# Second MoE block: six float32 weight pieces parked in DRAM, more of the small tensor work on VectorE, a new listed order

## The chip, the cores and the metric

The kernel runs on one core of a Trainium2 chip. TensorE (PE) multiplies, ScalarE (ACT), VectorE (DVE) and GpSimd (POOL) do the element-wise work, and SyncE (SP) issues every DMA in one queue. The metric is the device time of one execution in microseconds, the median over runs. For the kernel before it is 686.53 us (three runs, 686.2 to 686.76).

## The reference

Three blocks follow each other: a windowed attention over 2304 tokens (four sequences of 512 local and 32 global tokens, 8 heads of 64), a first MoE block (512 to 1024 to 512, softmax gate and layer norm), and the second block, which the change touches:

```python
def _moe2_ref(x, w_in, w_out):          # x (2304, 512), w_in (512, 2048), w_out (2048, 512)
    h = x @ w_in
    neg, pos = h <= -1.0, h >= 1.0
    g = np.where(pos, h, np.where(neg, 0.0, (h + 1.0) ** 2 / 4.0))
    return (g @ w_out).astype(np.float32)
```

## The kernel before

**Precision.** A float32 matrix is held as two parts: a high part, which ScalarE copies out in the matmul's own rounding, and a low part, the difference, which VectorE or GpSimd subtracts (`sub`, L835). A product is then three matmuls (`mm3`, L319): high by high, high by low, low by high. So each operand of TensorE needs one ScalarE copy and one or two subtractions first.

**Tiling of the second block.** The tokens form three blocks of 768, 768 and 640 (`BLOCKS`). The 2048 inner columns are 16 pieces `f` of 128 columns; each has an input weight `w2["i", f]` and an output weight `w2["o", f]`. For block 0 the pieces 0 to 7 are multiplied directly, each in two halves (`hprod`, L765; the loop over `k` at L1258). From piece 8 on, and for all of blocks 1 and 2, two pieces are taken together as a *pair* (`pair`, L902): a Strassen-Winograd scheme with seven products instead of eight. I write pair (b, p) for block b and pieces 2p and 2p+1. So there are four pairs in block 0, (0, 4) to (0, 7), and eight in each of the blocks 1 and 2. A pair needs

- four sums of token quarters, once per block (`ysum`, L840), with high and low parts (`yhigh`, `ylow`);
- four sums of weight quarters: `wfull` (L857) rebuilds the two float32 pieces into the tile `wt` by adding their high and low parts, `wsum` (L863) forms the sums in place, `whigh` and `wlow` split them into the tiles `S`. These sums are made once for each p, while the pair ahead of its first use runs, stored in DRAM (`wstore`) and loaded again for later blocks;
- seven products on two PSUM banks in turn, after which VectorE merges a product with earlier ones (`merge`, L929). The bank is free for the next product but one when its merge has read it. The activation is two ScalarE instructions and one on VectorE (`bend`, `least`), then the copy and the subtraction for `g`.

Between the seven products TensorE does the twelve accumulations `acc<-wo,g` of the pair before. The weights arrive as float64 words: each piece is fetched to `wraw` and converted by the steps A (ScalarE), B, D, F (VectorE) into the float32 tile `w32` (three buffers), then H (ScalarE) and L (VectorE or GpSimd) give its two parts (`conv`, L222).

**What sets the order.** The second block first lists its ScalarE, VectorE, GpSimd, DMA and matmul steps in `plan` (`later` appends). `ORDER`, a table of numbers at the head of the file, then calls them in a chosen order, so each engine's queue is in that order and each engine works in order. Which engine does a subtraction is fixed in the code before: GpSimd for `wfull`, `wlow`, nearly every low part of `g`, and the first four `ysum` (L1187), which are issued ahead of the plan.

Of the kernel before, what the change touches and what calls it, by code (L numbers as in the profile page):

```python
# [1439 lines left out]
```

## Time and profile before

| | us |
|---|---|
| median of three runs | 686.53 |
| the profiled execution | 686.77 |
| its span, first to last instruction | 684.6 |
| PE busy in the span | 655.7 (96%) |
| DVE, ACT, POOL busy | 446.7, 382.4, 277.1 |
| second block's direct stage, 301.89 to 363.29 | 61.40 |
| five pairs (0, 4) to (1, 0), 363.29 to 456.99 | 93.70 |

The profile is one execution. Times in it are counted from the span's start, and about 2.2 us of the execution lie outside the span. "Idle before <-" after an instruction is the time its engine stood still ahead of it and the engine that ended the wait. Neighbouring instructions of one engine overlap by some 0.07 us in the records, so from one start to the next is the better measure of what an instruction costs its queue. A pair is bounded here by the starts of its first product.

### The profile page before, as it was taken

The page shows a single profiled execution, that of the slowest core. Times are in us where ns is not written, and L with a number is a line of the kernel's source. Part 1 is how long each engine was busy: PE and PEld are TensorE (multiplying, and loading weights), DVE is VectorE, ACT ScalarE, POOL GpSimd, SP SyncE. Part 2 cuts the span into 40 slices and gives each one's busy share as a digit, 9 for nine tenths or more (in the row PEclk, how much of TensorE's full clock was granted, in tenths as well). Part 3 has the DMA queues.
Part 4 walks back from the last instruction along what each step waited for, and adds up shares of the span by engine and source line. Part 5 has one row for each costly group of instructions (what it writes and reads, how often), then busy time and mean ns, then how long its engine had stood idle before and what let it go on. Part 6 is the DMA issues. An engine that isn't in the chain of part 4 may idle for free.

```text
span 684.6 us, 15083 instructions
## 1 busy us (share of the span) xinstructions
PE 655.7 (96%) x6068; PEld 574.7 (84%) x6068; DVE 446.7 (65%) x746; ACT 382.4 (56%) x925; POOL 277.1 (40%) x286
## 2 busy tenths in 40 slices
PE   7699999999999999999999899799999999999997
PEld 4477889889898898989997788699998998988986
DVE  6998988785777499546999779955323353333332
ACT  5888886674564163428665556455434466444443
POOL 2243432141112143246677768866422254222321
PEclk9999999999999999999999999899999999999999
DMA  8999644336365335002574364244533335734512
GB/s 342 411 360 363 231 156 172 108 107 269 126 220 183 126 109 199 1 1 91 190 269 168 93 237 165 96 163 160 185 123 123 123 125 203 247 135 154 179 67 78
DMA packets 30837, 117.38 MB, mean 171 GB/s; under 512 B 3504, under 2 KB 4016, under 8 KB 28208
## 3 DMA queue, kind: packets, MB, share of 16 engines
q1 hardware_dynamic: 30768, 116.42, 47.6%
q8 instruction: 48, 0.79, 0.5%
q14 instruction: 21, 0.17, 0.1%
HBM read 92.03 MB, written 24.38 MB: 170 GB/s over the span
## 4 chain that ended last, share of the span: by engine, by line
PE 72%; DVE 12%; POOL 6%; issue 4%; DMA 3%; ACT 2%; SPq 0%; POOLq 0%; ACTq 0%; DVEq 0%
PE acc L324 19%; PE h L324 18%; PE h L583 12%; PE yT L324 10%; PE o L486 3%; PE S L405 2%; DVE xy L196 2%; DVE w L234 2%; PE pPT L471 2%; PE plnT L648 2%; POOL g L836 2%; DMA qkT<-in_qk_dram 2%; POOL S L836 1%; DVE w L236 1%; DVE w L232 1%
## 5 line engine op out<-in xcount | busy, mean ns | idle before, releaser
L324 PE MATMUL acc<-wo,g 128*128 128x512 f32 x816 | 214.6, 395 | 3.1 <-ACT o L205 3.1
L324 PEld LDWEIGHTS acc<-wo,g 128*128 128x128 f32 x816 | 150.3, 189 | 25.7 <-ACT o L205 3.4
L836 POOL TENSOR_TENSOR g<-xy,g 128x384 fp32r<-128x384 f32 (+2 forms) x95 | 92.4, 977 | 161.0 <-ACT g L205 135.5
L583 PE MATMUL h<-win,x 128*128 128x512 f32 x408 | 101.4, 400 | 1.1 <-issue 1.1
L205 ACT ACTIVATE xy<-xy 128x384 f32<-128x384 f32 (+1 forms) x148 | 74.7, 505 | 48.1 <-DVE xy L196 43.3
L324 PE MATMUL yT<-lnT,wout 128*128 128x256 f32 x768 | 95.7, 284 | 1.1 <-DVE lnT L196 1.0
L324 PEld LDWEIGHTS yT<-lnT,wout 128*128 128x128 f32 x768 | 92.9, 188 | 2.3 <-DVE lnT L196 1.5
L583 PEld LDWEIGHTS h<-win,x 128*128 128x128 f32 x408 | 74.8, 188 | 18.3 <-issue 1.9
L196 DVE SCALAR_TENSOR_TENSOR xy<-xy 128x384 f32<-128x384 f32 (+1 forms) x60 | 37.4, 623 | 51.3 <-ACT xy L205 51.3
L205 ACT ACTIVATE g<-xy 128x384 fp32r<-128x384 f32 (+1 forms) x88 | 44.3, 503 | 39.7 <-DVE xy L196 38.6
L196 DVE TENSOR_TENSOR xy<-h,xy 128x384 f32<-128x384 f32 (+1 forms) x80 | 42.2, 528 | 35.7 <-PE h L324 34.2
L324 PE MATMUL h<-yT,w2i 128*128 128x384 f32 (+1 forms) x324 | 61.9, 335 | 0.0
L324 PEld LDWEIGHTS h<-yT,w2i 128*128 128x128 f32 x324 | 57.2, 190 | 3.1
L324 PE MATMUL h<-yT,S 128*128 128x384 f32 (+1 forms) x240 | 46.5, 328 | 3.7 <-DVE xy L196 3.7
L205 ACT ACTIVATE xy<-h 128x384 f32<-128x384 f32 (+1 forms) x48 | 22.6, 470 | 48.9 <-PE h L324 48.8
L205 ACT ACTIVATE e<-S,nm 128x128 f32<-128x128 f32 x128 | 45.1, 380 | 7.6 <-DVE nm L196 5.7
L324 PE MATMUL h<-yc,S 128*128 128x384 f32 (+1 forms) x240 | 46.7, 330 | 1.7 <-DVE xy L196 1.4
L324 PEld LDWEIGHTS h<-yT,S 128*128 128x128 f32 x240 | 41.3, 188 | 8.1 <-DVE xy L196 4.8
L324 PEld LDWEIGHTS h<-yc,S 128*128 128x128 f32 x240 | 41.7, 191 | 6.3 <-DVE xy L196 3.0
L571 POOL TENSOR_TENSOR x<-xy,x 128x512 fp32r<-128x512 f32 x17 | 22.3, 1317 | 36.0 <-ACT x L205 29.9
L196 DVE SCALAR_TENSOR_TENSOR xy<-h,xy 128x384 f32<-128x384 f32 (+1 forms) x28 | 14.9, 534 | 30.9 <-ACT xy L205 30.9
L234 DVE SCALAR_TENSOR_TENSOR w<-wraw,w 128x512 int32<-128x512 int32 x38 | 33.5, 883 | 0.8
(153 smaller groups left out, 1042.4 us busy)
## 6 DMA issues: line engine op xcount, KB each, us to landing
vw<-in_vwin_dram SPq DMA_DIRECT2D x16, 1024.0 KB, 6.2
wo<-w2d_o SPq DMA_DIRECT2D x32, 512.0 KB, 4.1
S<-w2d_s SPq DMA_DIRECT2D x24, 512.0 KB, 5.1
qkT<-in_qk_dram SPq DMA_DIRECT2D x15, 768.0 KB, 7.0
wraw<-in_w2i_dram SPq DMA_DIRECT2D x16, 512.0 KB, 5.8
wraw<-in_w2o_dram SPq DMA_DIRECT2D x16, 512.0 KB, 4.1
w2d_o<-wo SPq DMA_DIRECT2D x16, 512.0 KB, 2.9
w2d_s<-S SPq DMA_DIRECT2D x16, 512.0 KB, 4.8
```

Of the source, the lines that this page charges most:

```text
L196: self.last = getattr(nc.vector, name)(*args, **kw)
L205: vec.act = nc.scalar.activation(**kw)
L232: return nc.vector.tensor_scalar(w.t, w.t, 3, None, ALU.logical_shift_left)
L234: return nc.vector.scalar_tensor_tensor(out=w.t, in0=w.high, scalar=SIGN, in1=w.t, op0=ALU.bitwise_and, op1=ALU.bitwise_or)
L324: mm(out=dst, lhsT=pairs[i][0][x], rhs=pairs[i][1][y], start=start and j == 0, stop=stop and j == 3 * n - 1, **kw)
L405: mm(out=S[32 * hp:32 * hp + 32, par, ci], lhsT=qT[r, hp, ci], rhs=kT[r, hp, w:w + 4].rearrange("p c d -> p (c d)"), start=True, stop=True)
L471: nc.tensor.transpose(ps[:, hp], eT[t][:, HP * par + hp], ident)
L486: mm(out=o[rows, ci, par], lhsT=PT[t][:, par, ci, rows], rhs=w[:, ci, D * h:D * h + D], start=True, stop=True)
L571: eng.tensor_tensor(out=xT[t][1], in0=x[:, :, n:n + P], in1=xT[t][0].bitcast(F32), op=ALU.subtract)
L583: mm(out=hps[t][:, half], lhsT=x[i][:, k], rhs=win[j][:, k, sl], start=not lo and j == 0 and k == 0, stop=lo and k == KD - 1)
L648: nc.tensor.transpose(ps[:, k], ln[t][:, P * c:P * c + P], ident)
L836: eng.tensor_tensor(out=out, in0=x, in1=y, op=ALU.subtract)
```

## The change

Four things change, all in the second block.

1. **Kept weights.** Input pieces of the sums that are converted inside the plan (10 to 15) have their float32 tile `w32` stored to DRAM after step F (`wkeep`). Where the sums of the pairs (0, 5), (0, 6) and (0, 7) are made, `wfetch` loads each piece into `wt` by one DMA of 256 KB instead of two GpSimd additions.
2. **A free choice of engine.** `ylow`, `wfull`, `wsum`, `wlow`, the low parts of `g` and of the weights are listed one instruction at a time, and an entry of `ORDER` may end in `v` (VectorE) or `p` (GpSimd).
3. **Whole halves.** In the direct stage the low part of `g` is one instruction of 128x384 instead of two of 128x192.
4. **The order.** A new table, and the four `ysum` of block 0 are entries of it.

On VectorE this gives 823 instructions instead of 740, on GpSimd 182 instead of 291, on SyncE 233 instead of 221. TensorE's order is the same row for row, and ScalarE has the same 767 instructions in another order.

```diff
 ORDER = """
-22 57 0 92 1 2 10 3 36 123 4 24 11 6 13 53 5 142 37 25 12 38 15 17 39 28 14 7 41 16 32 8 27 20 23 18 30 29 19
+25 60 4 95 5 6 0v 13 7 1v 9 109p 8 39 27 15 110p 14 18 10 17 16 40 11v 28 41 19 20 31 42 22 26 21v 44 36 30 32
...
-    def wfull(p, i):
+    def wfull(p, i, j, eng=nc.gpsimd):
         wt[p] = wts[0]
         a, b = w2["i", 2 * p + i]
-        for j in range(2):
-            nc.gpsimd.tensor_tensor(out=wt[p][:, 2 * i + j], in0=a[:, 2 * j:2 * j + 2].bitcast(F32), in1=b[:, 2 * j:2 * j + 2].bitcast(F32), op=ALU.add)
+        eng.tensor_tensor(out=wt[p][:, 2 * i + j], in0=a[:, 2 * j:2 * j + 2].bitcast(F32), in1=b[:, 2 * j:2 * j + 2].bitcast(F32), op=ALU.add)
+
+    def wfetch(p, i):
+        wt[p] = wts[0]
+        dma(out=wt[p][:, 2 * i:2 * i + 2].rearrange("p a k n -> p (a k n)"), in_=w2d["f", 2 * p + i])
+
+    def wkeep(f, w):
+        w2d["f", f] = dram.tile([P, 512], F32, name=f"w2d_f{f}")
+        dma(out=w2d["f", f], in_=w.tf)
+
+    def wfulls(p, i):
+        if 2 * p + i in kept:
+            return [partial(wfetch, p, i)]
+        return [partial(wfull, p, i, j) for j in range(2)]
...
         ysplit(0)
-        for i in (0, 3, 1, 2):
-            ysum(0, i, nc.gpsimd)
...
+        for i in (0, 3, 1, 2):
+            later(partial(ysum, 0, i))
...
-                for m in (slice(0, 192), slice(192, 384)):
-                    later(partial(lambda g, s, sl, m: sub(g()[1][:, sl][:, m], s[:, m], g()[0][:, sl][:, m].bitcast(F32), nc.gpsimd), gt[0, f], s, sl, m))
+                later(partial(lambda g, s, sl, eng=nc.gpsimd: sub(g()[1][:, sl], s, g()[0][:, sl].bitcast(F32), eng), gt[0, f], s, sl))
...
             for i in order:
-                plan[i]()
+                if i[-1] in "vp":
+                    plan[int(i[:-1])](eng=nc.vector if i[-1] == "v" else nc.gpsimd)
+                else:
+                    plan[int(i)]()
```

**The seam from the first to the second block, VectorE.** `e` is the first block's layer-norm tile of the last 128 tokens, `xy_88` the activations of block 0, `yT` their parts. Before:

```order
L196 TENSOR_REDUCE nm_4337<-h 128x1
L196 TENSOR_TENSOR yT_4359<-xy_88,yT_4358 128x768 x4
L196 TENSOR_SCALAR s_4340<-s_4340 128x1
L196 RECIPROCAL s_4340<-s_4340 128x1
L196 SCALAR_TENSOR_TENSOR e_4339<-e_4339,s_4340,h 128x1024
```

Now:

```order
L200 TENSOR_REDUCE nm_4337<-h 128x1
L200 TENSOR_TENSOR yT_4359<-xy_88,yT_4358 128x768 x3
L840 TENSOR_TENSOR xy_88<-xy_88 128x2x384
L200 TENSOR_TENSOR yT_4359<-xy_88,yT_4358 128x768
L200 TENSOR_SCALAR s_4340<-s_4340 128x1
L840 TENSOR_TENSOR xy_88<-xy_88 128x2x384
L200 RECIPROCAL s_4340<-s_4340 128x1
L200 SCALAR_TENSOR_TENSOR e_4339<-e_4339,s_4340,h 128x1024
```

Two of the four token sums, which stood on GpSimd, are now between VectorE's own rows here; the other two come later, in the direct stage.

**From pair (0, 7) to (1, 0), VectorE.** `h` is the PSUM bank, `xy_88` the room for the merged results, `xy_89` block 1. Before, from the merge of the sixth product (index 5) of (0, 7) to the first merge of (1, 0):

```order
L196 TENSOR_TENSOR xy_88<-h_5137,xy_88 128x384
L196 SCALAR_TENSOR_TENSOR xy_88<-xy_88 128x384
L196 TENSOR_TENSOR yc_1_4571<-xy_89,yc_0_4570 128x384 x2
L196 TENSOR_TENSOR xy_88<-h_5137,xy_88 128x384
L196 SCALAR_TENSOR_TENSOR xy_88<-xy_88 128x384
L196 TENSOR_TENSOR yT_4359<-xy_89,yT_4358 128x384 x2
L196 SCALAR_TENSOR_TENSOR xy_88<-xy_88 128x384
L196 TENSOR_TENSOR xy_89<-xy_90 128x640
L196 TENSOR_TENSOR xy_88<-h_5137,xy_88 128x384
```

Now, from the last merge of (0, 7) on:

```order
L200 TENSOR_TENSOR xy_88<-h_5106,xy_88 128x384
L840 TENSOR_TENSOR S_4832<-wt,S_4830 128x256
L840 TENSOR_TENSOR yc_1_4565<-xy_89,yc_0_4564 128x384
L840 TENSOR_TENSOR yT_4359<-xy_89,yT_4358 128x384
L840 TENSOR_TENSOR S_4832<-wt,S_4830 128x256
L840 TENSOR_TENSOR xy_89<-t_5624,xy_89 128x2x384
L200 TENSOR_TENSOR xy_88<-h_5106,xy_88 128x384
```

Low parts of `S` and `yc` have come over from GpSimd, and the sums for block 2 (128x640) have moved to later pairs.

**The fetches, SyncE.** `w2d_f` is a kept piece, `w2d_s` the stored sums, `wraw` the next words. Now, in the pairs (0, 4) and (0, 5):

```order
L867 DMA wt<-w2d_f_4885 128x512
L749 DMA w2d_o_5243<-wo 128x1024
L867 DMA wt<-w2d_f_4972 128x512
L899 DMA w2d_s_5264<-S_4831 128x1024
L899 DMA w2d_s_5264<-S_4833 128x1024
L749 DMA w2d_o_5291<-wo 128x1024
L277 DMA wraw<-in_w2o_dram 128x1024
```

The two fetches stand ahead of the store of the sums and of the next fetch of words, and the second one stands behind a store of output weights; before, this queue held no reads into `wt`.

## Rows read from the trace of the kernel before

**Rows 1.** The page, part 1: busy us, share of the span, instructions.
```profile
PE 655.7 (96%) x6068; PEld 574.7 (84%) x6068; DVE 446.7 (65%) x746; ACT 382.4 (56%) x925; POOL 277.1 (40%) x286
```

**Rows 2.** By stretch: length, busy PE PEld DVE ACT POOL, clock, DMA share, GB/s.
```profile
301.89:363.29 61.40, 61.40 (x314) 55.79 (x312) 49.79 (x70) 40.79 (x76) 42.96 (x45) 1.00 0.47 161
363.29:383.24 19.95, 16.55 (x79) 13.66 (x78) 18.69 (x27) 10.19 (x20) 14.08 (x16) 1.00 0.47 167
383.24:399.57 16.33, 16.11 (x79) 13.99 (x78) 12.27 (x17) 9.03 (x17) 12.15 (x13) 1.00 0.48 162
399.57:416.19 16.62, 15.92 (x79) 14.04 (x78) 12.93 (x21) 9.84 (x19) 12.31 (x13) 1.00 0.52 189
416.19:435.26 19.07, 16.52 (x79) 13.93 (x78) 18.97 (x23) 12.99 (x22) 16.57 (x14) 1.00 0.38 139
435.26:456.99 21.73, 18.62 (x79) 16.45 (x78) 15.57 (x22) 10.34 (x20) 13.13 (x14) 0.84 0.25 78
456.99:472.70 15.71, 15.71 (x79) 14.16 (x78) 9.51 (x14) 7.95 (x16) 11.47 (x14) 1.00 0.55 186
```

**Rows 3.** Whom PE waited for in the five pairs: us, times, longest.
```profile
PE h L324 <- DVE xy L196: 6.7, 6, 1.9
PE acc L324 <- ACT o L205: 3.1, 1, 3.1
```

**Rows 4.** Timeline of PE at the start of pair (1, 0).
```profile
442.01 1.65 PE L324 MATMUL acc<-wo,g 128*128 128x512 f32 x3 [3.11 <-ACT o L205]
443.46 2.12 PE L324 MATMUL h<-yT,w2i 128*128 128x384 f32 x6
```

**Rows 5.** Timeline of all engines at the seam: start, us, idle before.
```profile
274.50 0.81 DVE L196 TENSOR_SCALAR e<-e,mv,rstd 128x1024 f32<-128x1024 f32 x1 [0.73 <-POOL rstd L625]
...
284.48 11.55 PE L324 MATMUL yT<-lnT,wout 128*128 128x256 f32 x96
...
285.82 5.19 DVE L196 TENSOR_TENSOR yT<-xy,yT 128x768 fp32r<-128x768 f32 x4
...
287.71 6.92 POOL L836 TENSOR_TENSOR xy<-xy 128x768 f32<-128x768 f32 x3 [13.25 <-DVE yT L196]
...
295.10 1.82 POOL L836 TENSOR_TENSOR xy<-xy 128x768 f32<-128x768 f32 x1
295.17 2.30 DVE L196 TENSOR_SCALAR e<-e,mv,rstd 128x1024 f32<-128x1024 f32 x1 [0.83 <-POOL rstd L625]
...
297.62 1.06 PE L648 MATMUL plnT<-ident,e 128*128 128x128 f32 x8 [1.60 <-DVE e L196]
```

**Rows 6.** Timeline of DVE in pairs (0, 4) to (0, 7).
```profile
382.05 0.55 DVE L196 SCALAR_TENSOR_TENSOR xy<-xy 128x384 f32<-128x384 f32 x1
382.52 0.54 DVE L196 TENSOR_TENSOR xy<-h,xy 128x384 f32<-128x384 f32 x1
382.98 0.41 DVE L196 TENSOR_TENSOR wt<-wt 128x256 f32<-128x256 f32 x1
383.32 1.51 DVE L196 TENSOR_TENSOR wo<-w,wo 128x512 fp32r<-128x512 f32 x1
...
401.06 0.68 DVE L236 SCALAR_TENSOR_TENSOR w<-wraw,w 128x512 int32<-128x512 int32 x1
...
422.26 1.02 DVE L196 TENSOR_TENSOR xy<-xy 128x768 f32<-128x768 f32 x1
```

**Rows 7.** GpSimd in the five pairs, by form: busy us, mean ns.
```profile
L836 POOL TENSOR_TENSOR g<-xy,g 128x384 fp32r<-128x384 f32 x19 | 21.1, 1115 | 17.1 <-ACT g L205 17.0
L836 POOL TENSOR_TENSOR S<-wt,S 128x256 fp32r<-128x256 f32 x20 | 18.0, 928 | 6.4 <-ACT S L205 6.4
```

**Rows 8.** DMA issues from 300 to 460: KB each, us to landing.
```profile
out_dram<-o SPq DMA_DIRECT2D x6, 256.0 KB, 4.1
```

**Rows 9.** The same in the five pairs alone.
```profile
out_dram<-o SPq DMA_DIRECT2D x4, 256.0 KB, 2.0
```

**Rows 10.** ScalarE in the five pairs, by form: the copy of the sums.
```profile
L205 ACT ACTIVATE S<-wt 128x1024 fp32r<-128x1024 f32 x5 | 5.3, 1056 | 2.9 <-DVE wt L196 2.9
```

More of the change, by code (lines that the diff above doesn't have):

```diff
@@ new lines @@
+1051 1063 1055p 1058 1052 1057 1064 1060 1059 1061 1065 1062p 1067 1066 1068 1070 1069 1071 1072 1076 1073
+1075 1074v 1077 1078 1081 1079 1082 1080 1084 1083 1087 1088 1090 1085 1089v 1091 1086 1092 1095 1096 1098
+1093 1105 1097p 1100 1094 1099 1106 1102 1101 1103 1107 1104v 1109 1108 1110 1112 1111 1113 1114 1118 1115
+1117 1116p 1119 1120 1123 1121 1124 1122 1126 1125 1129 1130 1132 1127 1131v 1133 1128 1134 1137 1138 1140
+1135 1147 1139v 1142 1136 1141 1148 1144 1143 1145 1149 1146p 1151 1150 1152 1154 1153 1155 1156 1160 1157
@@ L104 @@
+1260 1264v 1267 1261 1272 1269 1268 1270 1273 1271v 1275 1274 1276 1278 1277 1279 1280 1284 1281 1283 1282v
+1285 1286 1289 1287 1290 1288 1291 1294 1295 1297 1292 1296v 1298 1293 1299 1302 1303 1305 1300 1304v 1309
+1301 1310 1306 1311 1307 1312 1308v 1320 1313 1321 1318 1314 1315 1322 1316 1323 1317 1319 1324 1329 1325 1330
+1326 1327 1331 1328
 """
@@ L848, in yhigh, with ylow, wsum, wlow @@
         act(out=yslot(b, i)[0], in_=ysource(b)[i], func=AF.Copy)
-    def ylow(b, i, eng):
+    def ylow(b, i, k, eng=nc.gpsimd):
         hi, lo = yslot(b, i)
-        for k in range(2):
-            sub(lo[:, k], ysource(b)[i][:, k], hi[:, k].bitcast(F32), eng)
+        sub(lo[:, k], ysource(b)[i][:, k], hi[:, k].bitcast(F32), eng)
     wt, wts = {}, []
-    def wfull(p, i):
+    def wfull(p, i, j, eng=nc.gpsimd):
         wt[p] = wts[0]
         a, b = w2["i", 2 * p + i]
-        for j in range(2):
-            nc.gpsimd.tensor_tensor(out=wt[p][:, 2 * i + j], in0=a[:, 2 * j:2 * j + 2].bitcast(F32), in1=b[:, 2 * j:2 * j + 2].bitcast(F32), op=ALU.add)
-    def wsum(p, i):
+        eng.tensor_tensor(out=wt[p][:, 2 * i + j], in0=a[:, 2 * j:2 * j + 2].bitcast(F32), in1=b[:, 2 * j:2 * j + 2].bitcast(F32), op=ALU.add)
[5 more added lines that the diff above has]
+        dma(out=w2d["f", f], in_=w.tf)
+    kept = set()
+    def wfulls(p, i):
+        if 2 * p + i in kept:
+            return [partial(wfetch, p, i)]
+        return [partial(wfull, p, i, j) for j in range(2)]
+    def wsum(p, i, eng=vec):
         a, b, c, d = (wt[p][:, j] for j in range(4))
         if i == 0:
-            tt(out=d, in0=c, in1=d, op=ALU.add)
+            eng.tensor_tensor(out=d, in0=c, in1=d, op=ALU.add)
         else:
-            sub(*((c, a, c), (a, d, a), (b, b, a))[i - 1])
+            sub(*((c, a, c), (a, d, a), (b, b, a))[i - 1], eng)
     def whigh(p):
         act(out=S[p % 2][0], in_=wt[p], func=AF.Copy)
-    def wlow(p, i):
-        for j in (2 * i, 2 * i + 1):
-            sub(*(a[:, j] for a in (S[p % 2][1], wt[p], S[p % 2][0].bitcast(F32))), nc.gpsimd)
+    def wlow(p, j, eng=nc.gpsimd):
+        sub(*(a[:, j] for a in (S[p % 2][1], wt[p], S[p % 2][0].bitcast(F32))), eng)
     def sflat(p, i):
@@ L899, in settle @@
             later(partial(lambda g, s: act(out=g()[0], in_=s, func=AF.Copy), g, s))
-            later(partial(lambda g, s: sub(g()[1], s, g()[0].bitcast(F32), eng), g, s))
+            later(partial(lambda g, s, eng=eng: sub(g()[1], s, g()[0].bitcast(F32), eng), g, s))
     def pair(b, p, items, extra):
@@ L1218, with keep @@
         for n in range(2):
-            early[8 + n].append(lambda n=n: wfull(P0, n))
-            early[11 + n].append(lambda n=n: wlow(P0, n))
-            early[14 + n].append(lambda n=n: wfull(P0 + 1, n))
+            early[8 + n].append(lambda n=n: wfulls(P0, n))
+            early[11 + n] += [partial(wlow, P0, 2 * n + j) for j in range(2)]
+            early[14 + n].append(lambda n=n: wfulls(P0 + 1, n))
         early[9].append(make_sums)
-        early[10] += [*(lambda n=n: wsum(P0, n) for n in range(4)), lambda: whigh(P0)]
+        early[10] += [*(partial(wsum, P0, n) for n in range(4)), partial(whigh, P0)]
         for k, i in ((2, 1), (4, 3), (6, 4)):
-            early[k].append(lambda i=i: yhigh(0, i))
-            early[k + 1].append(lambda i=i: ylow(0, i, nc.gpsimd))
+            early[k].append(partial(yhigh, 0, i))
+            early[k + 1] += [partial(ylow, 0, i, j) for j in range(2)]
         class Piece:
+            def keep(self):
+                io, f = self.key
+                if io == "i" and f >= 2 * P0:
+                    kept.add(f)
+                    later(lambda: wkeep(f, self.word))
             def first(self):
@@ L1249, in new_piece @@
             a = Piece()
+            a.key = io, j
             later(a.first)
@@ L1269 @@
                 if piece_low:
-                    later(partial(piece_low.step, "L", vec))
+                    later(partial(piece_low.step, "L", eng=vec))
                 if piece_now:
@@ L1287 @@
                 for op in early[k]:
-                    later(op)
+                    if isinstance(op, partial) or op is make_sums:
+                        later(op)
+                    else:
+                        plan.extend(op())
                 if f >= 2:
@@ L1309, in step, with ysteps @@
                     later(partial(a[0].step, "H"))
-                    later(partial(a[0].step, "L", low))
+                    later(partial(a[0].step, "L", eng=low))
+            def ysteps(b, c, i):
+                if c == "l":
+                    return [partial(ylow, b, i, j) for j in range(2)]
+                return [partial(yhigh if c == "h" else ysum, b, i)]
             jobs = [(0, p) for p in range(P0, K2 // 2)] + [(b, p) for b in range(1, len(BLOCKS)) for p in range(K2 // 2)]
@@ L1320 @@
                     if piece_low:
-                        extra[0].append(partial(piece_low.step, "L", nc.gpsimd))
+                        extra[0].append(partial(piece_low.step, "L", eng=nc.gpsimd))
                         piece_low = None
@@ L1333 @@
                     extra[2].append(partial(whigh, q))
-                    extra[3].append(partial(wlow, q, 0))
-                    extra[4].append(partial(wlow, q, 1))
+                    extra[3] += [partial(wlow, q, j) for j in range(2)]
+                    extra[4] += [partial(wlow, q, j) for j in range(2, 4)]
                 elif following[0]:
@@ L1338 @@
                 if following[1] in summed:
-                    extra[5] += [partial(wfull, following[1][1], i) for i in range(2)]
+                    extra[5] += [op for i in range(2) for op in wfulls(following[1][1], i)]
                 if (b, p) == (0, P0):
-                    extra[0].append(lambda: yhigh(0, 5))
-                    extra[1].append(lambda: ylow(0, 5, vec))
+                    extra[0].append(partial(yhigh, 0, 5))
+                    extra[1] += [partial(ylow, 0, 5, j) for j in range(2)]
@@ L1349 @@
                 if (b, p) == (1, 0):
-                    for i, op in ((0, lambda: ylow(1, 4, vec)), (0, lambda: yhigh(1, 5)), (0, lambda: yhigh(1, 6)),
-                                  (1, lambda: ylow(1, 5, vec)), (2, lambda: ylow(1, 6, nc.gpsimd))):
-                        extra[i].append(op)
+                    for i, c, j in ((0, "l", 4), (0, "h", 5), (0, "h", 6), (1, "l", 5), (2, "l", 6)):
+                        extra[i] += ysteps(1, c, j)
                 if b == 1 and 2 <= p < 6:
-                    extra[4].append(partial(ysum, 2, p - 2))
+                    extra[4] += ysteps(2, "s", p - 2)
@@ L1364 @@
                 op()
-        order = [int(i) for i in ORDER.split()] or range(len(plan))
+        order = ORDER.split() or [str(i) for i in range(len(plan))]
         with tc.manual_schedule(engines={mybir.EngineType.DVE, mybir.EngineType.Activation, mybir.EngineType.Pool}):
             for i in order:
-                plan[i]()
+                if i[-1] in "vp":
+                    plan[int(i[:-1])](eng=nc.vector if i[-1] == "v" else nc.gpsimd)
+                else:
+                    plan[int(i)]()
     w2bp.close()
```

57 lines of the change are left out of this document (50 added, 7 removed), and 49 rows, old and new, of the table ORDER.

## The prediction

> **What bounds the kernel now.** I began with the page: TensorE is busy for 655.7 of 684.6 us [rows 1], and the change leaves its order as it is. So nothing can be won in its work, only in its 29 us of idle time and in what that idle time brings on. Busy time by stretch shows where it lies [rows 2]. In the direct stage TensorE is busy for all of 61.40 us. A pair without a wait, (1, 1), takes 15.7 us. The five pairs ahead of it, (0, 4) to (1, 0), take 19.95, 16.33, 16.62, 19.07 and 21.73 us, which is 93.70 where 78.5 would do: 15.2 us too many, more than a reader should expect behind a 96% share.
>
> The view of waits names the releaser: in these pairs TensorE stood still 6.7 us for VectorE's merges and 3.1 us for ScalarE's copy of an accumulator [rows 3]. The rest follows from the stops. [...]
>
> Why is VectorE late? Its rows show it: an instruction of 128x512 takes 0.68 us in one place and 1.51 in another [rows 6]. The short ones are those beside which GpSimd rests. Taken from one start to the next, an undisturbed instruction costs 0.34 us at 256 columns, 0.47 at 384, 0.61 at 512 (0.68 less the overlap of 0.07), and 0.95 at 768 from the row of 1.02 [rows 6]; I take 0.33 for step B of a conversion, as for a plain 256, and 0.74 for 640, between its neighbours. By these prices VectorE's 106 rows in the five pairs (55 of 384, 19 of 256, 18 of 512, six steps B, four of 768, four of 640) need 52.2 us. They were busy for 78.4 [rows 2]. The 26.2 us between are spread over 68.2 us of busy GpSimd [rows 2]: each microsecond on GpSimd cost VectorE 0.38.
>
> **The seam of the two blocks.** GpSimd's four token sums go (6.92 and 1.82 us), and two come to VectorE ahead of the layer-norm tile `e`. Three things change there. The four low parts of `yT` took 5.19 us; two of them were done in 1.89, before GpSimd began at 287.71, so four undisturbed ones need about 3.8: 1.4 us less. Two sums of 768 add 2 x 0.95 = 1.9. The scaling of `e` took 2.30 us because the fourth sum ran beside it, and 0.81 one tile earlier: 1.5 less [rows 5, 6]. Together 1.0 us earlier. TensorE waited 1.60 us for this tile, and its work ahead lasts to 296.03 [rows 5], so it gets the whole of 1.0. Bounds: nothing, if the sums cost VectorE as much as they save, and 1.6, which is the wait itself.
>
> **The direct stage.** TensorE is never held there, so only a loss is possible. VectorE now has 82 instructions up to the last direct merge instead of 73. By the prices above they need 41.3 us instead of 36.8. Before, 13 us of contention came from 43 us of GpSimd, 0.30 each; now some 11 GpSimd instructions are left, about 11 us, so 3 us. 44.6 us in 61.40 leave 17 us of cover. The six stores of kept weights hold a `w32` tile longer, and a conversion three pieces later waits for it; I price this at nothing while the cover holds. Were it gone, each piece would push VectorE by up to one landing of 256 KB, 2.0 to 4.1 us [rows 8, 9], six times, 12 to 25 us against 17 of cover: 0 to 8 us on the path.
>
> **The five pairs.** Between the same merges VectorE's rows rise from 102 to 130. Now they are 69 of 384, 23 of 256, 26 of 512, eight steps B and four of 768: 32.4 + 7.8 + 15.9 + 2.6 + 3.8 = 62.5 us, 12 more than the 50.4 of before. GpSimd keeps 34 instructions, 24 of 256 and 10 of 384, at 0.93 and 1.12 us [rows 7] 33.5 us instead of 68.2. At 0.38 this costs VectorE 12.7 us instead of 26.2. Its sum is thus 75.2 us, a little less than the 78.4 of before, though it does 28 instructions more. By pairs I get 14.2, 13.9, 13.8, 17.0 and 16.5 us. Against 15.7 of TensorE the first three have air, (0, 7) exceeds it by 1.3 and (1, 0) by 0.8.
>
> Air is not enough by itself: (0, 5) and (0, 6) had VectorE busy for 12.27 and 12.93 us and still lost 0.63 and 0.92 [rows 2], since a merge arrives late when a long row stands ahead of it. I leave every pair that mean of 0.8. So 5 x 0.8 + 1.3 + 0.8 = 6.1 us are left of 15.2, and the gain is 9.1. [...]
>
> What hides the remaining lateness: a bank is needed two steps after its merge becomes possible. A step of a pair is 15.7 / 7 = 2.24 us, a product some 1.1, so a merge may come 3.4 us late at no cost.
>
> **The fetches.** In (0, 5) the last low parts of the old sums end about 1 us after the pair's start; behind them the second fetch is issued, lands 2.0 to 4.1 us later [rows 8, 9], then four `wsum` on GpSimd take 3.7 [rows 7] and the copy of `S` 1.06 [rows 10]. With the 4.1, to whose side I lean as its row has the queue loaded, and 0.4 for the issue, that is 10.3 us into the pair. VectorE's first low part of the new `S` waits for it, and behind that the merge of the fifth product, which ends at 4 x 2.24 + 1.1 = 10.1. So VectorE stops for 0.2 us, and TensorE asks for the next merge only at 13.4: 3 us of reserve. On SyncE the store of the sums and the next words queue behind the fetches; they have half a pair. I price it at nothing. The kept pieces save 12 additions, 11 us of GpSimd, which are in the sum above.
>
> [...]
>
> **Sum.** 686.77 for the profiled execution, less 1.0, less 9.1: 676.7. The median of the runs is 0.24 lower, so I say 676.5. Its own range: with a loss of 0.3 a pair and the excess hidden by the 3.4 us, 672; with 1.6 a pair and a share of 0.55 instead of 0.38 (2.7 more in the last two pairs), 683.
>
> **Rivals.**
> - *VectorE sets the pace.* It gets denser, and a GpSimd instruction now nearly always meets one of its rows. With 0.75 instead of 0.38 the pairs need about 16, 16.7, 15.6, 19.7 and 19.8 us and the 0.8 each: 91.8, a gain of 1.9, and 1.0 at the seam: 683.9. For it speaks that VectorE was saturated in (0, 4) and (0, 7); against it that the share was 0.30 in the direct stage, where VectorE was as dense. Range 682.5 to 686.5, chance 0.21.
> - *The fetch chain is late, slower.* Place: the first VectorE row of the new `S` in (0, 4), (0, 5) and (0, 6). It decides from the point where the chain exceeds its place by the 3.4 us; at 7.9 us late, which a second fetch held by the store ahead of it and landing behind two others would make, each of three pairs loses some 4.5: 13.5 more, 690. For it: the reserve is thin and the issue queue is in order. Against: DMA is at 0.38 to 0.52 there [rows 2]. Chance 0.12.
> - *GpSimd blocks VectorE wholly*, each microsecond for one: 96.0 us of work one after the other in the five pairs, 688.1. Chance 0.02, as the rows before don't bear it.
> - *All stops go*, the merges being early enough everywhere: 15.2 + 1.6 less, 670. Chance 0.05.
>
> My forecast has 0.60. A difference below 0.2%, 1.4 us, can't be told from no change here. Of the first rival I count 0.14 as faster, 0.05 as the same and 0.02 as slower; of the second 0.10 as slower and 0.02 as the same. Faster: 0.60 + 0.05 + 0.14 = 0.79; same 0.07; slower 0.14. The range 671 to 686 leaves out most of the two slower cases and half of the last.
>
> **What would show it.** Right: the wait of 1.60 us at the seam is 0.6 or less and `e` takes 0.81; the five pairs take 84 to 86 us, with VectorE busy for about 75 and GpSimd for about 34; rows of `S` and `g` on VectorE at 0.41 to 0.55 where GpSimd rests; a granted clock of 1.00 in pair (1, 0); the direct stage unchanged. Wrong: TensorE waiting in the direct stage, a wait of VectorE for a DMA into `wt` of more than 3 us, or lost time in pairs (1, 1) and (1, 2), which now get the sums for block 2.

## The result and the profile after

The changed kernel takes 668.58 us (median) beside 686.37 for the kernel before in the same runs: a ratio of 0.9748, 95% interval 0.9727 to 0.9768. The direction was right. The gain of 17.8 us is well above the 10 of the forecast, and the time lies 2.4 us below the range.

The page of the changed kernel, part 1, with the columns of [rows 1]:

```profile
PE 649.0 (97%) x6068; PEld 571.5 (86%) x6068; DVE 456.7 (69%) x829; ACT 380.6 (57%) x925; POOL 168.6 (25%) x177
```

GpSimd gave up 108.5 us and VectorE, with 83 instructions more, is busy for only 10 us more. TensorE has the same 6068 matmuls and is busy for 6.7 us less. Of this 5.5 us lie in the five pairs: 2.9 in (1, 0), where the clock was 0.84 before, and 2.6 in the other four, at a clock of 1.00: behind each of their nine gaps, short ones too, the first matmul takes 0.44 us instead of 0.34, and its overlap of some 0.16 us with the matmul ahead is gone. Another 1.0 us lies ahead of the direct stage.

The view by stretch, columns and stretches as in [rows 2], each from its first matmul to the next one's:

```profile
299.19:360.53 61.34, 61.34 (x312) 55.72 (x311) 46.86 (x83) 39.28 (x76) 10.13 (x10) 1.00 0.50 155
360.53:376.19 15.66, 15.66 (x79) 14.13 (x78) 14.16 (x27) 10.01 (x19) 5.47 (x6) 1.00 0.63 231
376.19:391.91 15.72, 15.72 (x80) 14.16 (x78) 12.89 (x24) 9.05 (x18) 8.15 (x8) 1.00 0.73 267
391.91:407.55 15.64, 15.64 (x80) 14.12 (x79) 13.86 (x26) 9.75 (x19) 5.70 (x6) 1.00 0.62 239
407.55:423.26 15.71, 15.71 (x79) 14.16 (x78) 14.68 (x27) 11.33 (x20) 6.29 (x6) 1.00 0.47 163
423.26:438.90 15.64, 15.64 (x80) 14.11 (x78) 14.22 (x30) 10.66 (x21) 5.42 (x6) 1.00 0.48 176
```

The first row is the direct stage, the others are the five pairs. In each TensorE's busy time equals the length: no stop is left, and the clock is 1.00 in all. They take 78.37 us; cut at the same matmuls those of before took 93.87, so 15.50 us were won. The view of waits has no line for TensorE from the seam to the end; [rows 3 and 4] have no counterpart. The direct stage kept its 61.34 us.

The timeline at the seam, beside [rows 5]:

```profile
283.52 11.55 PE L328 MATMUL yT<-lnT,wout 128*128 128x256 f32 x96
...
284.86 2.69 DVE L200 TENSOR_TENSOR yT<-xy,yT 128x768 fp32r<-128x768 f32 x3
287.46 0.95 DVE L840 TENSOR_TENSOR xy<-xy 128x768 f32<-128x768 f32 x1
...
289.26 0.94 DVE L840 TENSOR_TENSOR xy<-xy 128x768 f32<-128x768 f32 x1
290.32 1.28 DVE L200 SCALAR_TENSOR_TENSOR e<-e,s,h 128x1024 f32<-128x1024 f32 x1
...
294.08 0.81 DVE L200 TENSOR_SCALAR e<-e,mv,rstd 128x1024 f32<-128x1024 f32 x1 [0.73 <-POOL rstd L629]
...
295.04 1.06 PE L652 MATMUL plnT<-ident,e 128*128 128x128 f32 x8
```

The two sums stand among VectorE's own rows, with GpSimd at rest beside them; `e` takes 0.81 us instead of 2.30, and the tile's transposes follow without a wait. From the start of the 96 matmuls of `yT` to these transposes the kernel before took 13.14 us, this one 11.52: 1.62 won, the whole wait.

These two places make 17.1 us of the 18.2 by which the last matmul ends earlier. A further 0.96 us was there already at the start of the 96 matmuls, in work that the change doesn't touch; over the profiled runs of all kernels here that point lies between 281.6 and 285.1 us, so I don't count it as an effect. The last 0.1 us lies in the pairs behind.

### The profile page after: what moved, and what is told of

Read it like the earlier page. It is cut to its first block, busy times and chain, and to the rows that moved or that the text cites. A ratio compares the mean times of both kernels' runs of the same rounds, so it can differ in the third digit from the quotient of the medians.

```text
span 666.3 us, 14991 instructions
## 1 busy us (share of the span) xinstructions
PE 649.0 (97%) x6068; PEld 571.5 (86%) x6068; DVE 456.7 (69%) x829; ACT 380.6 (57%) x925; POOL 168.6 (25%) x177
## 4 chain that ended last, share of the span: by engine, by line
PE 90%; DVE 7%; issue 1%; ACT 1%; DMA 1%; SPq 0%; DVEq 0%; ACTq 0%
PE acc L328 28%; PE h L328 26%; PE h L587 13%; PE yT L328 12%; PE plnT L652 2%; PE o L490 2%; PE S L409 2%; PE pPT L475 2%; DVE w L240 1%; DVE w L238 1%; PE y L328 1%; DVE w L236 1%; DVE nm L200 1%; PE og L550 1%; ACT e L209 1%
## 5 line engine op out<-in xcount | busy, mean ns | idle before, releaser
L840 POOL TENSOR_TENSOR g<-xy,g 128x384 fp32r<-128x384 f32 (+1 forms) x38 | 38.0, 1001 | 147.1 <-ACT g L209 111.3
L200 DVE SCALAR_TENSOR_TENSOR xy<-xy 128x384 f32<-128x384 f32 (+1 forms) x60 | 34.4, 576 | 37.6 <-ACT xy L209 37.5
L200 DVE TENSOR_REDUCE nm<-h 128x1 f32<-128x1024 f32 x17 | 20.7, 1215 | 18.8 <-PE h L587 18.7
L840 DVE TENSOR_TENSOR g<-xy,g 128x384 fp32r<-128x384 f32 (+1 forms) x50 | 28.8, 582 | 5.4 <-ACT g L209 5.4
```

Of the source, the lines that this page charges most:

```text
L200: self.last = getattr(nc.vector, name)(*args, **kw)
L840: eng.tensor_tensor(out=out, in0=x, in1=y, op=ALU.subtract)
```

## The experiments

Two things are to be told apart: whether the merges are on time because VectorE is undisturbed (load), or because the new list places them better (order); and why the forecast got the size wrong. "Pairs" is the length of the five pairs in the run's own trace, which is one execution; times are medians, and each ratio is to the kernel before in the same rounds, whose median there lay between 684.87 and 686.37 us.

| run | pairs, us | time, us | ratio to before, 95% interval |
|---|---|---|---|
| before | 93.87 | 686.37 | 1 |
| changed | 78.37 | 668.58 | 0.9748 (0.9727 to 0.9768) |
| new order, old engines (e1) | 89.96 | 682.06 | 0.9964 (0.9946 to 0.9983) |
| changed, no kept weights (e2) | 79.95 | 671.34 | 0.9809 (0.9781 to 0.9837) |
| changed, old seam (e3) | 78.37 | 670.50 | 0.9791 (0.9763 to 0.9819) |
| changed, GpSimd rows twice (e4) | 86.17 | 677.71 | 0.9899 (0.9874 to 0.9925) |
| before, low parts of `S` on VectorE (e5) | 90.19 | 684.21 | 0.9976 (0.9952 to 1.0) |
| before, also additions and `g` (e6) | 87.68 | 680.62 | 0.9938 (0.9908 to 0.9967) |
| changed, merges repeated (e7) | 78.37 | 701.87 | 1.024 (1.0183 to 1.0296) |
| changed, both fetches twice (e8) | 93.90 | 682.58 | 0.9961 (0.9937 to 0.9985) |
| changed, one fetch twice (e10) | 85.74 | 675.50 | 0.9866 (0.9821 to 0.9912) |

**e1: the order without the engines.**

```diff
-                if i[-1] in "vp":
-                    plan[int(i[:-1])](eng=nc.vector if i[-1] == "v" else nc.gpsimd)
-                else:
-                    plan[int(i)]()
+                plan[int(i.rstrip("vp"))]()
```

> The changed kernel with its new listed order and its kept weights, but every low part, sum and merge on the engine that it had before: only the letters for VectorE and GpSimd are ignored. Load theory (VectorE's rows are late because GpSimd is busy beside them): GpSimd goes back to about 57 us in the five pairs (68.2 before, less some 11 for the kept pieces), VectorE to about 52 us of its own; at the 0.38 us per busy GpSimd us of before it would be busy for some 74 us, and the five pairs take 82 to 90 us instead of 78.4, so 672 to 680. Order theory (the merges now stand early enough, the engine of the rest doesn't matter): the pairs stay within 1 us of 78.4 and the time within 1 us of 668.6.

Pair (1, 0) by stretch:

```profile
432.47:452.14 19.67, 16.48 (x79) 13.93 (x78) 9.02 (x13) 9.77 (x20) 18.79 (x20) 1.00 0.37 133
```

The order, with the kept weights, won 3.9 of the 15.5 us: the order theory falls. The token sums of block 0 stayed on VectorE in this run, so it has the gain of the seam too. In (0, 7), which took 20.26 us, a merge of VectorE held TensorE for 2.70 us again; in the row shown GpSimd is busy for 18.79 of 19.67 us, and TensorE waited there 0.33 and 0.51 us for GpSimd's own rows beside 2.35 us for a merge. Over the five pairs GpSimd was busy for 66.3 us, where I expected 57, and VectorE for 66.7, where I expected 74; the time lies 2 us above the load theory's range.

**e4: the load without another order.** The operations of 23 GpSimd instructions run twice each:

```diff
+                if n in (0, 5):
+                    span.append(len(plan))
...
-                    plan[int(i[:-1])](eng=nc.vector if i[-1] == "v" else nc.gpsimd)
+                    f = plan[int(i[:-1])]
+                    twice = i[-1] == "p" and span[0] <= int(i[:-1]) < span[1] and (f.func in (ylow, wfull, wlow) or f.func.__name__ == "<lambda>")
+                    for _ in range(1 + twice):
+                        f(eng=nc.vector if i[-1] == "v" else nc.gpsimd)
```

> The changed kernel with 23 GpSimd instructions in the five pairs issued twice with the same operands (13 of 256 columns, 10 of 384), which adds 23.3 us to GpSimd's 31.0 and nothing to VectorE; the second one delays what waits for it by about 1 us. With the share of 0.235 VectorE's busy time goes from 69.8 to about 75.3 us in 78.4: nearly no stop, 668.6 to 671. With 0.38 it needs 83 us, so the pairs take 83 to 87 and the time is 673 to 677. Order theory (where the merges stand decides): no change, 668.6.

Pair (0, 6), and whom TensorE waited for in the five pairs:

```profile
393.72:414.48 20.76, 17.50 (x80) 15.14 (x79) 16.80 (x26) 9.87 (x18) 12.73 (x14) 0.92 0.60 215
```

```profile
PE h L328 <- DVE xy L200: 4.1, 4, 2.7
PE acc L328 <- POOL g L840: 0.5, 1, 0.5
```

With VectorE's rows and their order untouched, more work on GpSimd brought the stops back: the pairs are 7.8 us longer, 4.6 of it waits, the rest longer busy time of TensorE, 1.9 of it in (0, 6), whose clock of 0.92 follows the longest stop. So the order alone doesn't keep the merges on time. But there are two ways from GpSimd to a stop: by rows of VectorE that it hinders, and by work that waits for it. The larger part went the second way. Ahead of the stop of 2.71 us in (0, 6) VectorE stood idle:

```profile
402.71 0.66 ACT L234 ACTIVATE w<-wraw 128x512 f32<-128x512 f32 x1 [5.15 <-DMA wraw<-in_w2o_dram]
403.40 0.43 DVE L236 TENSOR_SCALAR w<-w 128x512 int32<-128x512 int32 x1 [3.30 <-ACT w L234]
```

ScalarE had to wait for the next words. Their fetch stood on SyncE behind two stores of `S`, whose low parts GpSimd now did twice; it was issued 1.78 us into the pair instead of 0.03 and landed 7.18 us later instead of 4.52. This pair lost 5.1 of the 7.8 us. For hindered rows at most the 2.7 us of the other pairs are left (0.3 in (0, 5), 1.7 in (0, 7), 0.7 in (1, 0)). That GpSimd's work brings stops is shown here; that they come from hindered rows is shown by (0, 5) in e5 and e2 below.

The pairs' length is in the range of the larger share, and the time 0.7 us above it. But VectorE was busy for 78.3 us, not 83, which makes a share of 0.31 (78.3 less 62.5 by the prices, over 50.3 us of GpSimd), between the two; the changed kernel's own trace gives 0.235 (69.8 less 62.5, over 31.0).

**e9: which rows are hindered.** Forms of VectorE, 12 rows each, alone and beside additions on GpSimd:

```diff
+        "two SBUF": lambda: vec.tensor_tensor(out=z, in0=x, in1=y, op=ALU.add),
+        "PSUM and SBUF": lambda: vec.tensor_tensor(out=z, in0=h, in1=y, op=ALU.add),
+        "one SBUF": lambda: vec.tensor_scalar(z, x, 0.5, None, ALU.mult),
+        "one SBUF copy": lambda: vec.tensor_copy(u, w),
```

> A measurement by itself, not the kernel (its output is zeros): 12 VectorE rows of one form, alone and then beside 13 GpSimd additions of 128x256 with both operands in SBUF, for four forms: 384 columns with two SBUF operands; 384 with one operand in PSUM and one in SBUF; a multiply of 384 with one SBUF operand; a copy of 512 with one SBUF operand. Theory that any two rows of VectorE and GpSimd hinder each other (the one share of 0.38 for all rows that the prediction used): all four forms get longer, 0.55 to about 0.75 or more. Theory from the traces (merges out of PSUM took 0.55 us whether or not GpSimd ran beside them, rows with SBUF operands alone 0.8 to 1.0 instead of 0.42 to 0.55): the form with a PSUM operand stays at 0.55, that with two SBUF operands goes to 0.85 to 1.1. For the forms with one SBUF operand the traces leave both open.

VectorE's timeline (start, busy us of the whole group of 12); L69 to L72 are the four forms, each first alone and then beside GpSimd:

```profile
5.79 7.07 DVE L69 TENSOR_TENSOR z<-x,y 128x384 f32<-128x384 f32 x12
...
13.92 11.51 DVE L69 TENSOR_TENSOR z<-x,y 128x384 f32<-128x384 f32 x12
...
28.92 7.06 DVE L70 TENSOR_TENSOR z<-h,y 128x384 f32<-128x384 f32 x12
...
37.04 7.06 DVE L70 TENSOR_TENSOR z<-h,y 128x384 f32<-128x384 f32 x12
...
49.67 4.70 DVE L71 TENSOR_SCALAR z<-x 128x384 f32<-128x384 f32 x12
...
55.42 9.17 DVE L71 TENSOR_SCALAR z<-x 128x384 f32<-128x384 f32 x12
...
68.09 5.57 DVE L72 COPY u<-w 128x512 f32<-128x512 f32 x12
...
74.05 9.91 DVE L72 COPY u<-w 128x512 f32<-128x512 f32 x12
```

GpSimd's rows beside them (L89, in the same order of forms) and alone at the end (L97):

```profile
15.13 11.68 POOL L89 TENSOR_TENSOR gc<-ga,gb 128x256 f32<-128x256 f32 x12
...
38.01 9.55 POOL L89 TENSOR_TENSOR gc<-ga,gb 128x256 f32<-128x256 f32 x12
...
56.44 9.54 POOL L89 TENSOR_TENSOR gc<-ga,gb 128x256 f32<-128x256 f32 x12
...
75.13 10.21 POOL L89 TENSOR_TENSOR gc<-ga,gb 128x256 f32<-128x256 f32 x12
...
88.00 9.54 POOL L97 TENSOR_TENSOR gc<-ga,gb 128x256 f32<-128x256 f32 x12
```

The rows with an operand in PSUM take 7.06 us with and without GpSimd beside them, and GpSimd keeps its 9.55. With two operands in SBUF both engines pay: VectorE 4.44 us, GpSimd 2.14. With a single operand, in SBUF, VectorE pays as much (4.47 and 4.34 us) and GpSimd little (0 and 0.67). So it isn't a busy GpSimd that costs, but GpSimd beside a row with all its operands in SBUF.

The same split in the kernels, worked out over the five pairs from the start and the length of every row (excess: length less the tenth percentile of its form over all these runs; lengths are added up, so GpSimd's is a little over its busy time):

| run | GpSimd busy | beside PSUM rows: overlap, excess | beside SBUF-only rows: overlap, excess |
|---|---|---|---|
| before | 70.3 | 11.8, 0.1 | 49.8, 24.6 |
| changed | 32.0 | 10.3, 0.3 | 17.9, 6.3 |
| e4 | 50.9 | 13.9, 0.2 | 36.9, 16.0 |
| e5 | 51.7 | 8.5, 0.2 | 38.4, 20.3 |

The merges are PSUM rows; with 0.1 to 0.3 us of excess over 8.5 to 13.9 us of overlap they are late by what stands ahead of them, not by themselves. Per us of overlap with the other rows 0.35 to 0.53 us are lost in these four runs (0.65 in e6 below, which has only 13.3 us of such overlap). Of GpSimd's time 71% lay beside such rows before and 56% after; that and the lower loss per us make the share smaller than its 0.38. In e4 the added instructions fell almost all beside such rows.

**e5 and e6: the engines without the order.** e5 is the middle edit; e6 has all three:

```diff
-            nc.gpsimd.tensor_tensor(out=wt[p][:, 2 * i + j], ...
+            vec.tensor_tensor(out=wt[p][:, 2 * i + j], ...
...
-            sub(*(a[:, j] for a in (S[p % 2][1], wt[p], S[p % 2][0].bitcast(F32))), nc.gpsimd)
+            sub(*(a[:, j] for a in (S[p % 2][1], wt[p], S[p % 2][0].bitcast(F32))))
...
-    def settle(eng=nc.gpsimd):
+    def settle(eng=vec):
```

> The kernel before, in its own order, with one edit: the low parts of the weight sums S (20 rows of 128x256 in the five pairs, four more in the direct stage) go from GpSimd to VectorE, at the place in the order that they have. VectorE's own work in the five pairs rises from 52.2 to 59.0 us, GpSimd's falls from 68.2 to about 50. Load theory, with 0.53 us lost for each us in which GpSimd runs beside a VectorE row whose operands all lie in SBUF (from the first four runs): such overlap falls from 47 to some 33 us, VectorE's busy time from 82 to 80 or 81, and the pairs from 93.9 to 86 to 93 us: 679 to 686. Order theory: the same merges behind more rows, so slower, 687 to 692.

> The kernel before, in its own order, with the low parts of S, the additions of kept and unkept weights and the low parts of g in all pairs on VectorE: 12 rows of the direct stage and about 60 of the five pairs leave GpSimd. VectorE's own work in the five pairs rises from 52.2 to about 75 us of 78.4, GpSimd keeps about 10 us. Load theory: 75 and some 4 us of contention, so VectorE is full, and the pairs with the most rows stop TensorE: pairs 80 to 88 us, time 673 to 681. Theory that any rows added to VectorE in this order make its merges later: 686 or more.

By stretch, (0, 5) of e5:

```profile
381.56:397.26 15.70, 15.70 (x80) 14.14 (x78) 12.21 (x22) 9.20 (x18) 8.56 (x9) 1.00 0.47 169
```

Pairs (0, 4), (0, 5) and (0, 7) of e6:

```profile
360.29:379.72 19.43, 16.77 (x79) 13.85 (x78) 18.94 (x39) 10.63 (x20) 4.57 (x5) 1.00 0.48 175
379.72:395.41 15.69, 15.69 (x79) 14.14 (x78) 13.69 (x30) 9.34 (x19) 1.29 (x1) 1.00 0.49 169
...
411.38:432.23 20.85, 17.70 (x79) 15.15 (x78) 20.33 (x34) 13.40 (x23) 6.49 (x6) 0.92 0.27 102
```

Both times lie in the load theory's ranges, though e5's ratio can hardly be told from 1. Pair (0, 5) is the telling one. In the old order, with 22 and 30 rows of VectorE where there were 17, it no longer loses anything; before it lost 0.63 us [rows 2]. The steps B, D and F of a conversion stand there ahead of the merge that was late, before with GpSimd beside them:

```profile
387.46 1.24 DVE L232 TENSOR_SCALAR w<-w 128x512 int32<-128x512 int32 x1
388.73 1.11 DVE L234 SCALAR_TENSOR_TENSOR w<-wraw,w 128x512 int32<-128x512 int32 x1
389.88 1.11 DVE L236 SCALAR_TENSOR_TENSOR w<-wraw,w 128x512 int32<-128x512 int32 x1
```

The same three in e5, where GpSimd has no low parts of `S` to do:

```profile
385.72 0.49 DVE L232 TENSOR_SCALAR w<-w 128x512 int32<-128x512 int32 x1
386.24 0.69 DVE L234 SCALAR_TENSOR_TENSOR w<-wraw,w 128x512 int32<-128x512 int32 x1
386.97 0.69 DVE L236 SCALAR_TENSOR_TENSOR w<-wraw,w 128x512 int32<-128x512 int32 x1
```

More rows didn't make its merges late; GpSimd had. In (0, 6) the old order has a part of its own: of the 0.92 us of before, 0.7 are still lost in e5 and 0.3 in e6. VectorE stands idle there until ScalarE has the next words (2.36 us before, 1.31 in e5), and the new list issues their fetch 0.03 us into the pair instead of 2.25.

But (0, 4) and (0, 7) stay full: by the prediction's prices e6 puts 16.6 and 16.9 us of VectorE's own work into pairs of 15.7. The new list puts 12.4, 11.4, 11.4, 13.7 and 12.6 into the five, where the old one had 12.5, 7.7, 9.0, 12.4 and 10.4. Engines alone, as e6 allots them, won 6.2 us in the pairs of its trace (4.9 by the medians, as the traced execution was its fastest) and order alone 3.9; neither gives the 15.5. That a lighter GpSimd and evenly spread rows of VectorE together do is argued from these prices: the new kernel's own choice of engines in the old order was not run.

**e2 and e3: the kept weights, and the seam.**

```diff
-        wt[p] = wts[0]
-        dma(out=wt[p][:, 2 * i:2 * i + 2].rearrange("p a k n -> p (a k n)"), in_=w2d["f", 2 * p + i])
+        for j in range(2):
+            wfull(p, i, j)
...
-        w2d["f", f] = dram.tile([P, 512], F32, name=f"w2d_f{f}")
-        dma(out=w2d["f", f], in_=w.tf)
+        pass
```

> The changed kernel without the kept weights: no store of the float32 pieces, and each fetch replaced by the two additions on GpSimd, at the fetch's place in the order. GpSimd gets 12 additions of 128x256, some 11 us more, over the six that the fetches stand for. Load theory with the share of the changed kernel's trace (7.3 us of VectorE time lost beside 31.0 us of GpSimd, 0.235): VectorE 72.4 us in 78.4, no stop, 668.6 to 669.5. With the 0.38 of the prediction: 78 to 79 us, two or three pairs stop, 671 to 673. Theory that the fetches themselves make the difference (the additions delay the chain up to the new sums): the merge of the fifth product comes late in each of three pairs, 673 to 680.

TensorE's only stop in the five pairs without kept weights:

```profile
384.00 1.32 PE L328 MATMUL h<-yc,S 128*128 128x384 f32 x6 [1.30 <-DVE xy L200]
```

One pair, (0, 5), lost 1.6 us, and the others nothing: the kept pieces are a small part, about 1.6 us of the 15.5. The time is in the range of the larger share, but one pair stopped, not two or three, and VectorE was busy for 75.5 us in the pairs, between the two shares. The stop doesn't come from the chain up to the new sums: their copy began 9.4 us after the pair's start instead of 7.6, at 386.00, when the stop was over. From the pair's start to the late merge VectorE had no break. Its last rows, and the merge (`xy<-h,xy`):

```profile
380.23 2.10 DVE L840 TENSOR_TENSOR g<-xy,g 128x384 fp32r<-128x384 f32 x2
...
382.25 1.22 DVE L248 TENSOR_TENSOR wo<-w,wo 128x512 fp32r<-128x512 f32 x1
383.40 0.55 DVE L200 TENSOR_TENSOR xy<-h,xy 128x384 f32<-128x384 f32 x1
```

The same rows in the changed kernel, where GpSimd rests until 379.51:

```profile
378.39 1.02 DVE L840 TENSOR_TENSOR g<-xy,g 128x384 fp32r<-128x384 f32 x2 [0.38 <-ACT g L209]
379.34 0.68 DVE L248 TENSOR_TENSOR wo<-w,wo 128x512 fp32r<-128x512 f32 x1
379.94 0.55 DVE L200 TENSOR_TENSOR xy<-h,xy 128x384 f32<-128x384 f32 x1
```

In the same order of VectorE, the merge began 6.82 us into the pair instead of 3.75, behind rows up to twice as long (they make 2.6 of the 3.1 us), and TensorE stopped: here hindered rows make the stop.

```diff
+        for i in (0, 3, 1, 2):
+            ysum(0, i, nc.gpsimd)
...
-            later(partial(ysum, 0, i))
+            later(lambda eng=None: None)
```

> The changed kernel with the four token sums of block 0 back on GpSimd, ahead of the listed order, as before; all else as changed. If the seam is worth what the traces show there (the wait of 1.60 us for the tile e is gone), 670.2 and the wait is back; if it is worth the 1.0 us of the prediction's working, 669.6; if the sums in the direct stage were also a load there, a little more.

The end of the seam in e3:

```profile
294.29 2.30 DVE L200 TENSOR_SCALAR e<-e,mv,rstd 128x1024 f32<-128x1024 f32 x1 [0.82 <-POOL rstd L629]
...
296.73 1.06 PE L652 MATMUL plnT<-ident,e 128*128 128x128 f32 x8 [1.58 <-DVE e L200]
```

The wait is back, the way to the transposes takes 13.13 us instead of 11.52, and all that follows is as in the changed kernel: the seam is worth 1.6 us. The medians can't show so little: they come from different rounds, and the ratios' intervals touch.

**e7: how late a merge may be.**

```diff
+    LATE = {(1, 2, 1): 6, (1, 3, 3): 6, (1, 4, 1): 12, (1, 5, 3): 12, (1, 6, 3): 18}
...
-                later(partial(merge, i, r))
+                later(lambda i=i, r=r, times=LATE.get((b, p, i), 1): [merge(i, r) for _ in range(times)])
```

> The changed kernel with one merge done several times over, with the same operands and result, in each of five pairs of block 1 where GpSimd hardly runs: the merge of the second product 6 times in (1, 2) and 12 times in (1, 4), of the fourth product 6 times in (1, 3), 12 times in (1, 5) and 18 times in (1, 6). Each repeat takes 0.47 us, so the merges come 2.35, 5.2, 2.35, 5.2 and 8.0 us later. By the prediction (a merge may come 3.4 us late at no cost) TensorE waits 0, 1.8, 0, 1.8 and 4.6 us. By the code the fourth product's bank is used again by the fifth product, one step on, with 1.1 us of other work between, so its merge may come only 1.1 us late: 0, 1.8, 1.2, 4.1 and 6.9. If a stop of some us brings the lower clock with it, as after the stop of 3.11 us before, the pair (1, 6) loses 2 to 3 us more than it waits.

Three of TensorE's five stops, which lie behind the five pairs of the table:

```profile
483.14 1.33 PE L328 MATMUL h<-yc,w2i 128*128 128x384 f32 x6 [2.23 <-DVE xy L200]
501.46 2.29 PE L328 MATMUL h<-yc,S 128*128 128x384 f32 x6 [4.79 <-DVE xy L200]
...
555.42 2.29 PE L328 MATMUL h<-yc,lnT 128*128 128x384 f32 x6 [9.32 <-DVE xy L200]
```

A repeat takes 0.59 us (six take 3.52), not 0.47, so the merges came 2.96, 2.96, 6.5, 6.5 and 10.0 us later. Less the stops of 1.25, 2.23, 4.79, 5.79 and 9.32 us: the second product's merge may come 1.7 us late at no cost, both times, and the fourth's 0.7, three times. The 3.4 us of the prediction are wrong. In e2 the second product's merge came 3.07 us later than in the changed kernel, which less the stop of 1.30 leaves 1.8, as here. After the last three stops `h` takes 2.29 us, and the granted clock of these pairs is 0.85, 0.86 and 0.82; their busy time is 17.96, 18.25 and 18.48 us where 15.7 would do, so each of these stops cost 2.3 to 2.8 us beyond itself, as the one at 442 us did before [rows 4], where the pair's clock was 0.84. After the stops of 1.25 and 2.23 us `h` takes 1.32 and 1.33 us, at a clock of 1.00.

**e8 and e10: the reserve of the fetches.** e8 has `range(2)`, e10 `range(1 + i)`, so that only the later fetch is doubled:

```diff
-        dma(out=wt[p][:, 2 * i:2 * i + 2].rearrange("p a k n -> p (a k n)"), in_=w2d["f", 2 * p + i])
+        for _ in range(1 + i):
+            dma(out=wt[p][:, 2 * i:2 * i + 2].rearrange("p a k n -> p (a k n)"), in_=w2d["f", 2 * p + i])
```

> The changed kernel with each fetch of a kept piece into wt done twice, one behind the other, so that the chain fetch, sums, copy, low parts starts 2 to 4 us later in (0, 4), (0, 5) and (0, 6). By the prediction's reserve of about 3 us nothing to 1 us is lost at each of three places: 668.6 to 671. Theory that the chain is already at its limit, as the 1.7 us that the run without kept weights lost in (0, 5) may mean: 2 to 4 us at each, 674 to 680.

> The changed kernel with only the later of the two fetches of each pair done twice, so that the second copy waits for the first one's landing, some 3 us, once in each of (0, 4), (0, 5) and (0, 6). With the prediction's reserve of 3 us: at most 1 us lost in all, 668.6 to 670. With the reserve of 1.3 to 1.9 us that the run with both fetches doubled suggests (there a copy of the sums that was 2.8, 4.7 and 6.5 us later cost 1.5, 5.2 and 8.8 us): 1 to 2 us in each of two or three pairs, 671 to 675.

e8, SyncE's waits from (0, 4) to (0, 6), and (0, 6) by stretch:

```profile
SPq L868 <- DMA wt<-w2d_f: 15.7, 5, 4.6
```

```profile
399.19:423.66 24.47, 19.83 (x79) 16.80 (x78) 14.11 (x27) 9.97 (x20) 5.95 (x6) 0.79 0.61 219
```

e10, TensorE's stops in (0, 5) and (0, 6):

```profile
390.78 1.32 PE L328 MATMUL h<-yT,S 128*128 128x384 f32 x6 [1.58 <-DVE xy L200]
400.59 1.32 PE L328 MATMUL h<-yc,S 128*128 128x384 f32 x6 [1.20 <-DVE xy L200]
405.66 2.29 PE L328 MATMUL h<-yc,lnT 128*128 128x384 f32 x6 [2.37 <-DVE xy L200]
```

Both times lie above what I expected. My expectation for e8 missed what the first row says: five times the second copy isn't issued before the first has landed, and SyncE's queue stands for 3.1 us in the mean, with the next words behind it. All of the gain in the pairs was lost. Part of this is the words and not the sums: in (0, 4) of e8 VectorE stood idle for 4.98 us until ScalarE had them, in (0, 6) of e10 for 2.10 us, behind 3.32 us for the fetch itself. In e10, with the copies of the sums 1.0, 3.2 and 4.4 us later than in the changed kernel, the pairs lost 0, 1.9 and 5.5 us (2.0 of the last at the lower clock, by its busy time of 17.61). In (0, 5) of e10 VectorE waits 2.54 us for the copy of the sums ahead of the stop of 1.58; this leaves that pair a reserve of 1.6 us, not 3, and e8 gives 1.6 too (2.8 us later, a stop of 1.2).

## Why the prediction was right and wrong

- **The bound and the mechanism: right.** The stops, the clock of 0.84 in (1, 0) and the cause, VectorE's rows hindered by GpSimd, are as read from the profile; e5 and e2 show it row by row in (0, 5). The profile of before has a second cause beside it, which the prediction didn't read: ahead of the stop in (0, 6) VectorE waited 2.36 us for words.
- **The residual of 0.8 us a pair, 4.0 in all: the step that failed first.** I read it in (0, 5) and (0, 6) as a mishap of the order, a long row ahead of a merge. Such rows were long because of GpSimd (1.24, 1.11 and 1.11 us for B, D and F, in e5 0.49, 0.69 and 0.69), which the sum had already charged. e5 and e6 show it: same order, more rows, less GpSimd, no loss in (0, 5). There it was counted twice. In (0, 6) some 0.3 to 0.7 of the 0.92 us did belong to the old order, which fetched the words late; the new order fetches them earlier. In the changed kernel the term measures nothing in all five pairs.
- **The share of 0.38: mis-sized.** VectorE was busy for 69.8 us in the pairs, not 75.2, at 31.0 us of GpSimd, not 33.5. The excess of 1.3 and 0.8 us in (0, 7) and (1, 0) didn't come about: they have 14.68 and 14.22 us, not 17.0 and 16.5. Not all of that is the share: with the rows and the GpSimd time that these pairs had (13.7 and 12.6 us of VectorE's own, 6.29 and 5.42 us of GpSimd) even 0.38 gives 16.1 and 14.7, so the prediction also put too much work into them. A share per busy us couldn't be carried to another order, 0.38 before and 0.235 after; e9 shows what it depends on. I spread the share over all rows alike, and the rival of whole blocking adds up all rows alike. The form with an operand in PSUM took 7.06 us in e9 with GpSimd beside it and without, so the 29 PSUM rows of the pairs should have been left out of either sum.
- **The seam: 1.0 forecast, 1.6 measured**, its upper bound. I charged 0.5 us net for the two sums among the low parts; from the first low part to the row `e<-e,s,h` it took 5.46 us, against 5.49 in e3, so they cost nothing, and the 1.5 of `e` remained.
- **The cover of 3.4 us: wrong, without harm.** It is 1.7 or 0.7 us; in the changed kernel nothing came that late.
- **The direct stage and the fetches: the price of nothing was right**, 61.34 us both times and no wait in the pairs. The direct stage's share was nearer 0.55 than 0.30 (46.86 us busy less 41.3, over 10.13 of GpSimd), which the cover hid. And the fetches' chain was saved by an earlier start, not by its reserve: in (0, 5) the fetch was issued 0.31 us after the pair's start, where I had 1 to 1.4, it landed 2.9 us later, where I leaned to 4.1, and the sums were copied at 7.6 us, where I had 9.25. With the copy at 10.8, in e10, that pair stops.
- **The rivals.** "All stops go", 670 at a chance of 0.05, is what happened; of what lies beyond it, 1.9 us in the profiled executions, 0.96 is the earlier start ahead of the seam. "The fetch chain is late, slower" is a real mechanism. That its price came near, 15.5 us lost in the five pairs of e8 where I had 13.5, is luck: part of e8's loss came by way of the words, which that rival doesn't name, and it took copies of the sums 2.8 to 6.5 us later than they were. "VectorE sets the pace" and whole blocking fall with VectorE's 12.9 to 14.7 us in pairs of 15.7.

The profiled execution took 668.1 us, 8.6 less than the sum's 676.7. The residual is 4.0 of it, the excess 2.1, the seam 0.6, the earlier start 0.96, and 0.3 that the five pairs had more to lose than the 15.2 I counted; the last 0.6 lie behind the pairs and outside the span. With the measured gains in the two terms the same sum gives 686.8 less 15.5 less 1.6: 669.7.
